# Sigmoid attention with a top-1 mixture of experts on one core: one program order for all engines through attention, and early loads spread over three queues

## The chip, the cores and the metric

The kernel runs on one core of a Trainium2 chip. The metric is the device time of one execution in microseconds (us). The kernel before took 952.7 us, the median of three executions (951.31, 952.70, 954.98). A further execution was taken with the profiler on; all rows of the trace quoted below are from that one.

A core has five engines that run their own instruction streams: TensorE (PE, with its weight loads listed as PEld), VectorE (DVE), ScalarE (ACT), GpSimd (POOL) and SyncE (SP). Each runs its stream in order and waits on semaphores for the others. SP, ACT and POOL can start DMAs; all these DMAs run on the same 16 DMA engines.

## The reference

```
# q, k, v: 8 batches x 12 heads x 448 rows x 64
scores = q @ k.T / sqrt(64) - log(448)
attn   = sigmoid(scores)
x      = (attn @ v), heads side by side: 3584 tokens x 768
# mixture of experts, 8 experts, top 1
logits = x @ w_gate                      # 768 x 8
e      = argmax(logits);  gate = softmax(logits)[e]
out    = gate * (relu(x @ w1[e]) @ w2[e])    # w1: 768 x 1024, w2: 1024 x 768
```

All is float32. Where accuracy matters, a float32 factor is split into a rounded part and its rest ("h" and "l"), and three of the four products are summed.

## The kernel before, in words

**Attention** handles pairs of heads: 8 batches of 6 pairs, 48 pairs. Two pairs make a round of 7 steps (`ST`), so there are 168 steps `s`, and `u, i = divmod(s, 7)`. At an even step, PE runs the products of attention weights and values that are due (`weighted`, L504) and then the scores of two steps (`scores`, L484). Each score tile is turned into attention weights by a sigmoid on ACT (`squash`, L476), four score tiles being in flight. At the end of a round two finished output tiles are copied by ACT and DVE into the pair `xh`, `xl` (L530, L531).

**Loads.** `load_pair` (L429) starts eight DMAs for a pair, four for k and four for q. `load_values` (L445) starts three: the tile `vn` and two pieces of `ve`. `turn` (L457) transposes k or q on DVE. The table `READY` (L541) says at which step of a round each of these is called; loads of k and q are called about twelve steps before use. Rings of tiles (4 for k and for q, 3 for `vn`) bound how far a load can run ahead.

**Gate and tokens.** When a batch's 21 steps (`PB`) are done, its gate is worked out in pieces over the next steps (`gate_a` to `gate_e`), the number of the batch's most frequent expert is read into SP's registers (`load_regs`, L384), and `tokens` (L391) writes the batch's x to the DRAM tensor `x_tok` in two halves of four DMAs, from a staging tile `xt` that has one buffer.

**Experts, first part.** All tokens of a batch are run through that batch's most frequent expert (`moe`, L192). This is 288 matmuls for a batch. From step `START` = 33 on, 14 of them are put among the matmuls of each attention step. The weights come as raw tiles (`wst`, ring of 5, loaded by SP) which ACT rounds (`w1h`, `w2h`) and POOL subtracts (`w1l`, `w2l`); `Weights.ahead(n)` (L171) issues the loads and splits up to part `n`.

**Experts, second part.** The tokens whose own expert is another one are gathered after attention, run through their experts in a loop, and scattered to the output (L628 on).

**What sets the order.** The tile framework normally orders each engine's stream itself, by a model of when things are ready. `tc.manual_schedule(engines=...)` takes engines out of this: their streams keep the order in which the source calls them. Before, PE keeps source order through all of attention, DVE and ACT only up to step 3 (`ORDERED_TO`); after that, DVE, ACT, POOL and SP are ordered by the framework. The work after attention is ordered by the framework up to the last loops.

Of the kernel before, what the change touches and what calls it, by code (L numbers as in the profile page):

```python
# [10 lines left out]
F32 = mybir.dt.float32  # L11
# [4 lines left out]
AF = mybir.ActivationFunctionType  # L16
# [3 lines left out]
P = 128  # L20
NCH = 4
# [4 lines left out]
def tile_sigmoid_attention_top1_moe(  # L26
# [18 lines left out]
    nc = tc.nc  # L45
    B, H, S, D = q.shape
    NT, DM = out.shape
    E = w_gate.shape[1]
    DF = w1.shape[2]
    NP = H // 2  # L50
    KD = DM // P
# [8 lines left out]
    recs = dram.tile([E * NT, 2], U32, name="recs")  # L60

    const = ctx.enter_context(tc.tile_pool(name="const", bufs=1))
# [40 lines left out]

    wgs = const.tile([P, KD, 2 * E], F32R, name="wgs")

    def setup():
        wg = const.tile([P, KD, E], F32, name="wg")
        nc.sync.dma_start(wg, w_gate.rearrange("(t p) e -> p t e", p=P))
        nc.scalar.copy(wgs[:, :, 0:E], wg)
        nc.vector.tensor_sub(wgs[:, :, E : 2 * E], wg, wgs[:, :, 0:E].bitcast(F32))  # L110
        blank = wpool.tile([P, 1024], U32, tag="wst", bufs=RAWS_AHEAD, name="blank")
        blank3 = blank[:, : E * NT // P * 2].rearrange("p (r w) -> p r w", w=2)
        for w, val in enumerate((int(BIG), 0)):
            nc.gpsimd.iota(blank3[:, :, w], pattern=[[0, E * NT // P]], base=val, channel_multiplier=0)
        nc.sync.dma_start(recs.rearrange("(p r) w -> p r w", p=P), blank3)

    def apart(put, puts):
        for other in puts:
# [143 lines left out]
    def gate_b(b):  # L262
        pl = small_ps(b, "pl")
        for c in range(NCH):
            nc.tensor.transpose(
                pl[:, c * 2 * E : (c + 1) * 2 * E], g16[:, c * P : (c + 1) * P], ident[: 2 * E, : 2 * E]
            )
        plv = pl[:, : NCH * 2 * E].rearrange("p (c n e) -> p c n e", n=2, e=E)
        sh = [P, NCH, E]

        def tl(nm, shape=sh, dt=F32):
            return small.tile(shape, dt, tag=nm, name=f"{nm}_{b}")

        def bc(a):
            return a.unsqueeze(2).broadcast_to(sh)

        lg = tl("lg")
        nc.vector.tensor_copy(lg, plv[:, :, 0])
        nc.vector.tensor_add(lg, lg, plv[:, :, 1])
        mx = tl("mx", [P, NCH])  # L280
        nc.vector.tensor_reduce(mx, lg, axis=AX.X, op=ALU.max)
        eq = tl("eq")
        nc.vector.tensor_tensor(eq, lg, bc(mx), op=ALU.is_equal)
        nc.vector.tensor_tensor(eq, eq, rev.unsqueeze(1).broadcast_to(sh), op=ALU.mult)
        mr = tl("mr", [P, NCH])
        nc.vector.tensor_reduce(mr, eq, axis=AX.X, op=ALU.max)
        oh = tl("oh", sh, BF16)
        nc.vector.tensor_tensor(oh, eq, bc(mr), op=ALU.is_equal)
        nc.vector.memset(oh[S - 3 * P :, 3], 0.0)
        z = tl("z")  # L290
        nc.vector.tensor_tensor(z, lg, bc(mx), op=ALU.subtract)
        s1 = tl("s1")
        nc.scalar.activation(s1, z, AF.Sigmoid)
        s2 = tl("s2")
        nc.scalar.activation(s2, z, AF.Sigmoid, scale=-1.0)
        return oh, s1, s2

    def gate_c(b, oh, s1, s2):
        def tl(nm, shape, dt=F32):
            return small.tile(shape, dt, tag=nm, name=f"{nm}_{b}")  # L300

        pc = small_ps(b, "pc")
        nc.tensor.matmul(pc[:, : NCH * E], ones, oh.rearrange("p c e -> p (c e)"), start=True, stop=True)
        cnt = tl("cnt", [P, E])
        nc.vector.tensor_reduce(cnt, pc[:, : NCH * E].rearrange("p (c e) -> p e c", e=E), axis=AX.X, op=ALU.add)
        cm = tl("cm", [P, 1])
        nc.vector.tensor_reduce(cm, cnt, axis=AX.X, op=ALU.max)
        ce = tl("ce", [P, E])
        nc.vector.scalar_tensor_tensor(ce, cnt, cm, rev, op0=ALU.is_equal, op1=ALU.mult)
        cr = tl("cr", [P, 1])  # L310
        nc.vector.tensor_reduce(cr, ce, axis=AX.X, op=ALU.max)
        ri = tl("ri", [P, 1], I32)
        nc.vector.tensor_scalar(ri[:, 0:1], cr, -1.0, float(E), op0=ALU.mult, op1=ALU.add)
        nc.vector.tensor_scalar(ce, ce, cr, None, op0=ALU.is_equal)
        nc.vector.reciprocal(s2, s2)
        nc.vector.tensor_mul(s1, s1, s2)
        sm = tl("sm", [P, NCH])
        nc.vector.tensor_reduce(sm, s1, axis=AX.X, op=ALU.add)
        nc.vector.tensor_scalar(sm, sm, 1e-9, None, op0=ALU.add)
        nc.vector.reciprocal(gates[:, b], sm)  # L320

        nc.vector.tensor_scalar(ce, ce, -1.0, 1.0, op0=ALU.mult, op1=ALU.add)
        lm = tl("lm", [P, NCH, E], BF16)
        nc.vector.tensor_tensor(lm, oh, ce.unsqueeze(1).broadcast_to([P, NCH, E]), op=ALU.mult)
        return ri, lm
# [83 lines left out]
    def small_ps(b, name):  # L409

        return ps_moe.tile([P, 512], F32, tag="moe", name=f"{name}_{b}")
# [17 lines left out]
    def load_pair(g):  # L429
        if g >= NG:  # L430
            return
        b, hp = divmod(g, NP)
        for nm, src in (("k", k), ("q", q)):
            t = apool.tile([P, S // 32, 32], F32, tag=nm + "n", bufs=4, name=f"{nm}n_{g}")
            eng = nc.scalar if (g, nm) == (0, "q") else nc.sync
            for h in range(2):
                for f in range(D // 32):
                    a = 2 * h + f
                    eng.dma_start(  # L439
                        t[32 * a : 32 * (a + 1)],  # L440
                        src[b, 2 * hp + h, :, 32 * f : 32 * (f + 1)].rearrange("(j r) s -> r j s", r=32),
                    )
            ops[g, nm + "n"] = t
# [21 lines left out]
    def warm_up(n):  # L465

        ps = ps_moe.tile([P, 512], F32, tag="moe", name="ps_warm")
        for _ in range(n):
            nc.tensor.matmul(ps[:, :P], ones, ones, start=True, stop=True)
# [61 lines left out]
            nc.vector.tensor_sub(xl, pv[:, :S], xh.bitcast(F32))  # L531
            xch[divmod(g, NP)] = (xh, xl)

    WARM, V_POOL = 76, 3
    START = 33
    PB = NP // 2 * ST
    ET = mybir.EngineType
    ORDERED_TO = 3
    MIX = (7, 7)

    READY = {  # L541
# [7 lines left out]
    def attention():  # L549

        order = ExitStack()
        order.enter_context(tc.manual_schedule(engines={ET.PE}))
        first = order.enter_context(ExitStack())
        first.enter_context(tc.manual_schedule(engines={ET.DVE, ET.Activation}))
        warm_up(WARM)
        load_pair(0)
        load_pair(1)
        turn(0, "k")
        turn(0, "q")
        load_values(0)  # L560
        for g in (2, 3, 4):
            load_pair(g)
        pend_gate = None
        done_av = 0
        for s in range(N_ST + 11 + KD):
            u, i = divmod(s, ST)
            if s == 6:
                setup()
            if s == ORDERED_TO:
                first.close()  # L570
            if s % 2 == 0:


                while done_av < min(s - (s < START), N_ST):
                    weighted(done_av)
                    done_av += 1
                    if done_av % ST == 0:
                        break
                for n in range(s, min(s + 2, N_ST)):
                    scores(n)  # L580
            yield s, MIX[0]
            if i in READY and s < N_ST:
                READY[i](u)
            gb = s - PB
            if gb >= 0:
                b, r = divmod(gb, PB)
                r -= 3 if b == 0 else 2
                at = ("a", "b", None, "c", "l", "d", "e") if b == 0 else ("a", "b", "c", "l", "d", "e")
                what = at[r] if 0 <= r < len(at) else None
                if what == "a":  # L590
                    gate_a(b)
                elif what == "b":
                    pend_gate = gate_b(b)
                elif what == "c":
                    pend_gate = gate_c(b, *pend_gate)
                    gate_out[b] = pend_gate[0]
                elif what == "l":
                    load_regs(b)
                    if b == 0:
                        wts.ahead(2)  # L600
                elif what == "d":
                    gate_d(b, *pend_gate)
                elif what == "e":
                    gate_e(b)
                if 7 <= r < 7 + KD:
                    tokens(b, r - 7)
            yield s, MIX[1]
        order.close()

    wts = Weights([(lambda b=b: regs.get(b)) for b in range(B)])  # L610
# [310 lines left out]
```

## Time and profile before

| what | us |
|---|---|
| median of three executions | 952.7 |
| the profiled execution | 959.16 |
| its span, first to last instruction | 957.4 |
| PE busy in it | 897.4 |
| POOL, ACT, DVE busy | 407.2, 385.7, 350.1 |
| first matmul of the experts (L208) | 96.70 after the start |

The profile has these views: a page with the busy time of each engine and its granted clock over the span; a timeline, in which equal instructions in a row are merged, with the idle time of the engine before them in square brackets and what ended it; groups of instructions with count, busy time and mean; waits by engine, summed, with count and longest; and windows, which give each engine's busy time in chosen stretches, with the granted clock of TensorE as a share of full speed, the mean busy share of the DMA engines and the rate of the data moved. A name such as `at<-sc,bias_s` reads "writes at from sc and bias_s".

### The profile page before, as it was taken

The numbers are of one execution on the slowest core, as the hardware profiler recorded it, in microseconds if no ns is written. First come the engines' busy times: TensorE is split into PE (matmuls) and PEld (weight loads), VectorE is DVE, ScalarE is ACT, GpSimd is POOL, SyncE is SP. The second block draws the span as 40 slices with busy tenths as digits, with TensorE's granted clock in tenths as the row PEclk, the third lists the DMA queues.
The fourth block names the chain that finished last, engine by engine and source line by source line (L and its number), as shares of the span: only waits on it lengthen the run. The fifth ranks groups of instructions, "written<-read, shape, count | busy, mean of one in ns | idle before, by whom it ended". The sixth has DMA issues, their size and how long they took to land.

```text
span 957.4 us, 13357 instructions
## 1 busy us (share of the span) xinstructions
PE 897.4 (94%) x4470; PEld 624.7 (65%) x4470; DVE 350.1 (37%) x730; ACT 385.7 (40%) x690; POOL 407.2 (43%) x362
## 2 busy tenths in 40 slices
PE   9778999999999999997999999999999999997986
PEld 5223667666656767665766766767666678996786
DVE  3335333621352324621334323513352325136354
ACT  4444453325233443343333633435343532313344
POOL 3002431835056523653047613743255508967130
PEclk9778999999999999998999999999999999998898
DMA  9667862755437653955347653946353405529414
GB/s 128 118 121 173 163 155 55 184 122 161 79 90 148 134 137 65 190 100 158 59 112 146 153 116 75 201 106 149 60 150 91 139 1 147 161 56 301 148 43 140
DMA packets 319250, 120.47 MB, mean 126 GB/s; under 512 B 222596, under 2 KB 314212, under 8 KB 319184
## 3 DMA queue, kind: packets, MB, share of 16 engines
q1 hardware_dynamic: 310512, 106.34, 48.2%
q0 software_dynamic: 6816, 13.07, 5.5%
q8 instruction: 35, 0.57, 0.3%
q10 hardware_dynamic: 1856, 0.23, 0.2%
q14 instruction: 31, 0.25, 0.1%
HBM read 97.55 MB, written 24.64 MB: 128 GB/s over the span
## 4 chain that ended last, share of the span: by engine, by line
PE 53%; DMA 7%; DVE 3%; issue 2%; ACT 2%; SPq 1%; POOL 1%; POOLq 0%; DVEq 0%; ACTq 0%
PE ps L229 18%; PE ps L208 12%; PE av L515 6%; PE sc L492 6%; PE ps L797 6%; DMA wst<-in_moe_w_dram 5%; PE psg L256 1%; PE sc L500 1%; PE av L524 1%; DMA x_tok<-xt 1%; DMA w2r<-in_moe_w_dram 1%; DMA w1r<-in_moe_w_dram 1%; SPq L439 1%; POOL w2l L144 0%; ACT w2h L143 0%
## 5 line engine op out<-in xcount | busy, mean ns | idle before, releaser
L478 ACT ACTIVATE at<-sc,bias_s 128x448 f32<-128x448 f32 x336 | 187.6, 636 | 234.9 <-PE sc L492 208.2
L144 POOL TENSOR_TENSOR w2l<-wst,w2h 128x512 fp32r<-128x512 f32 x96 | 123.9, 1307 | 279.1 <-ACT w2h L143 217.6
L144 POOL TENSOR_TENSOR w1l<-wst,w1h 128x768 fp32r<-128x768 f32 x64 | 117.2, 1841 | 158.5 <-ACT w1h L143 157.7
L229 PE MATMUL ps<-hh,w2h 128*128 128x448 f32 x384 | 144.1, 375 | 7.4 <-DVE gt L381 2.7
L208 PE MATMUL ps<-xh,w1h 128*128 128x448 f32 x384 | 142.9, 372 | 8.0 <-DVE hl L214 8.0
L492 PE MATMUL sc<-qt,kt 64*128 64x448 f32 x576 | 141.4, 598 | 5.8 <-ACT at L478 5.3
L515 PE MATMUL av<-at,vn 128*64 128x448 f32 x576 | 134.7, 582 | 12.2 <-DVE xl L531 11.1
L229 PE MATMUL ps<-hl,w2h 128*128 128x448 f32 x384 | 143.4, 373 | 0.0
L229 PE MATMUL ps<-hh,w2l 128*128 128x448 f32 x384 | 142.1, 370 | 0.6 <-POOL w2l L144 0.6
L208 PE MATMUL ps<-xl,w1h 128*128 128x448 f32 x384 | 142.1, 370 | 0.0
L208 PE MATMUL ps<-xh,w1l 128*128 128x448 f32 x384 | 141.8, 369 | 0.0
L492 PEld LDWEIGHTS sc<-qt,kt 64*128 64x128 f32 x576 | 67.7, 254 | 84.1 <-issue 63.1
L214 DVE SCALAR_TENSOR_TENSOR hl<-ps,hh 128x448 fp32r<-128x448 f32 x64 | 39.8, 622 | 196.6 <-ACT hh L213 196.6
L143 ACT CAST w2h<-wst 128x512 fp32r<-128x512 f32 x96 | 57.6, 621 | 99.4 <-PE ps L229 58.7
L229 PEld LDWEIGHTS ps<-hh,w2h 128*128 128x128 f32 x384 | 75.0, 195 | 21.4 <-issue 9.0
L208 PEld LDWEIGHTS ps<-xh,w1h 128*128 128x128 f32 x384 | 72.3, 188 | 23.6 <-DVE hl L214 10.0
L515 PEld LDWEIGHTS av<-at,vn 128*64 128x64 f32 x576 | 37.4, 142 | 76.5 <-issue 52.0
L229 PEld LDWEIGHTS ps<-hh,w2l 128*128 128x128 f32 x384 | 75.0, 195 | 12.0 <-issue 5.5
L229 PEld LDWEIGHTS ps<-hl,w2h 128*128 128x128 f32 x384 | 75.0, 195 | 9.7 <-issue 6.2
L143 ACT CAST w1h<-wst 128x768 fp32r<-128x768 f32 x64 | 53.5, 836 | 68.8 <-DMA wst<-in_moe_w_dram 25.1
L208 PEld LDWEIGHTS ps<-xh,w1l 128*128 128x128 f32 x384 | 72.1, 188 | 13.2 <-issue 7.5
L208 PEld LDWEIGHTS ps<-xl,w1h 128*128 128x128 f32 x384 | 72.4, 189 | 12.6 <-issue 7.1
(148 smaller groups left out, 907.7 us busy)
## 6 DMA issues: line engine op xcount, KB each, us to landing
wst<-in_moe_w_dram SPq DMA_DIRECT2D x64, 384.0 KB
wst<-in_moe_w_dram SPq DMA_DIRECT2D x48, 512.0 KB
kn<-in_k_dram SPq DMA_DIRECT2D x192, 56.0 KB
x_tok<-xt SPq DMA_DIRECT2D x64, 168.0 KB
out_dram<-ob POOLq DMA_DIRECT2D x96, 112.0 KB, 3.2
qn<-in_q_dram SPq DMA_DIRECT2D x188, 56.0 KB
vn<-in_v_dram SPq DMA_DIRECT2D x45, 192.0 KB
w1r<-in_moe_w_dram SPq DMA_DIRECT2D x12, 512.0 KB
```

Of the source, the lines that this page charges most:

```text
L143: nc.scalar.copy(hi, st)
L144: eng.tensor_tensor(lo, st, hi.bitcast(F32), op=ALU.subtract)
L208: nc.tensor.matmul(ps[:, :S], a[:, ws], b_, start=(t == 0 and n == 0), stop=(t == KD - 1 and n == 2))
L214: nc.vector.scalar_tensor_tensor(hl[:, :S], ps[:, :S], 0.0, hh[:, :S].bitcast(F32), op0=ALU.max, op1=ALU.subtract)
L229: nc.tensor.matmul(ps[:, :S], a, b_, start=(j == 0 and n == 0), stop=(j == KF - 1 and n == 2))
L256: nc.tensor.matmul(psg[: 2 * E, :S], wgs[:, t], xch[b, t][n], start=(t == 0 and n == 0), stop=(t == KD - 1 and n == 1),)
L439: eng.dma_start(t[32 * a : 32 * (a + 1)], src[b, 2 * hp + h, :, 32 * f : 32 * (f + 1)].rearrange("(j r) s -> r j s", r=32),)
L478: nc.scalar.activation(at, ps[:, :S], AF.Sigmoid, bias=bias_s, scale=SCALE)
L492: nc.tensor.matmul(pss[h][:, :S], ks, ops[g, "q"][OWN[h]], start=True, stop=True)
L500: nc.tensor.matmul(pss[n][quarter(g, h), :S], ops[g, "k"][OWN[h], KB:], ops[g, "q"][OWN[h]], start=True, stop=True,)
L515: nc.tensor.matmul(psv[g][OWN[h], :S], ops[g, "v"][0][:, h, c, :], ats.pop((g, c, h)), start=(c == 0), stop=False)
L797: nc.tensor.matmul(*a, **kw)
```

## The change

From the start of attention to its end, the streams of all engines keep the order of the source. Around this, some calls change place or engine:

- the gate weights `wg` are loaded by POOL right after the first pair loads are called, and split on POOL (copy and subtract) at step 6; before, SP loaded them at step 6, ACT made the copy and DVE the subtraction;
- the blank records are written by a DMA from POOL in place of SP;
- the two sigmoids of the gate move from `gate_b` to `gate_c`, which is called one or two steps later;
- q of pairs 0 and 1 is loaded from ACT's queue (before: of pair 0);
- values of pairs 0 to 9 are loaded from POOL (before: 0 to 2);
- at step 28 only the first raw weight tiles are loaded (`ahead(0)`), and the first two parts are split at step 32 (`ahead(2)`); before, both stood at step 28.

```diff
+    wg = const.tile([P, KD, E], F32, name="wg")
+
     def setup():
-        wg = const.tile([P, KD, E], F32, name="wg")
-        nc.sync.dma_start(wg, w_gate.rearrange("(t p) e -> p t e", p=P))
-        nc.scalar.copy(wgs[:, :, 0:E], wg)
-        nc.vector.tensor_sub(wgs[:, :, E : 2 * E], wg, wgs[:, :, 0:E].bitcast(F32))
+        nc.gpsimd.tensor_copy(wgs[:, :, 0:E], wg)
+        nc.gpsimd.tensor_sub(wgs[:, :, E : 2 * E], wg, wgs[:, :, 0:E].bitcast(F32))
...
-        nc.sync.dma_start(recs.rearrange("(p r) w -> p r w", p=P), blank3)
+        nc.gpsimd.dma_start(recs.rearrange("(p r) w -> p r w", p=P), blank3)
...
-        s1 = tl("s1")
-        nc.scalar.activation(s1, z, AF.Sigmoid)
-        s2 = tl("s2")
-        nc.scalar.activation(s2, z, AF.Sigmoid, scale=-1.0)
-        return oh, s1, s2
-
-    def gate_c(b, oh, s1, s2):
+        return oh, z
+
+    def gate_c(b, oh, z):
...
+        s1, s2 = tl("s1", [P, NCH, E]), tl("s2", [P, NCH, E])
+        nc.scalar.activation(s1, z, AF.Sigmoid)
+        nc.scalar.activation(s2, z, AF.Sigmoid, scale=-1.0)
...
-            eng = nc.scalar if (g, nm) == (0, "q") else nc.sync
+            eng = nc.scalar if g < Q_ACT and nm == "q" else nc.sync
...
-    WARM, V_POOL = 76, 3
+    WARM, V_POOL, Q_ACT = 76, 10, 2
...
-        order.enter_context(tc.manual_schedule(engines={ET.PE}))
-        first = order.enter_context(ExitStack())
-        first.enter_context(tc.manual_schedule(engines={ET.DVE, ET.Activation}))
+        order.enter_context(tc.manual_schedule())
...
+        nc.gpsimd.dma_start(wg, w_gate.rearrange("(t p) e -> p t e", p=P))
...
-            if s == ORDERED_TO:
-                first.close()
+            if s == START - 1:
+                wts.ahead(2)
...
-                        wts.ahead(2)
+                        wts.ahead(0)
```

More of the change, by code (lines that the diff above doesn't have):

```diff
@@ L532, in weighted @@
             xch[divmod(g, NP)] = (xh, xl)
-    WARM, V_POOL = 76, 3
+    WARM, V_POOL, Q_ACT = 76, 10, 2
     START = 33
     PB = NP // 2 * ST
-    ET = mybir.EngineType
-    ORDERED_TO = 3
     MIX = (7, 7)
```

## The prediction

> **What bounds the kernel now.** I read the page first, for the share of PE.
>
> ```profile
> span 957.4 us, 13357 instructions
> ...
> PE 897.4 (94%) x4470; PEld 624.7 (65%) x4470; DVE 350.1 (37%) x730; ACT 385.7 (40%) x690; POOL 407.2 (43%) x362
> ```
>
> PE sets the time and no other engine is near its limit, so only two things can be won: stretches in which PE has nothing to do, and stretches in which it runs at a lower clock. The windows view, cut at PE's gaps, shows where these lie.
>
> ```profile
> core 0: us, PE busy (x) PEld busy (x) DVE busy (x) ACT busy (x) POOL busy (x), PEclk, DMA share, GB/s
> 0.00:28.40 28.40, 26.36 (x166) 14.41 (x166) 11.30 (x24) 13.08 (x23) 8.11 (x25) 1.00 0.87 126
> 28.40:33.70 5.30, 0.03 (x2) 0.02 (x1) 0.21 (x1) 0.84 (x3) 0.00 (x0) 0.69 0.72 142
> 33.70:59.00 25.30, 25.30 (x114) 9.03 (x114) 7.41 (x13) 15.54 (x30) 0.00 (x0) 0.86 0.59 106
> 59.00:66.00 7.00, 0.07 (x4) 0.04 (x2) 1.22 (x3) 1.57 (x3) 0.00 (x0) 0.65 0.78 158
> 66.00:86.20 20.20, 19.31 (x89) 7.56 (x89) 11.04 (x44) 6.98 (x14) 0.00 (x0) 0.87 0.60 113
> 86.20:96.70 10.50, 6.62 (x21) 2.25 (x21) 3.87 (x7) 5.86 (x11) 6.58 (x6) 0.67 1.11 263
> 96.70:860.00 763.30, 741.37 (x3629) 521.63 (x3628) 267.62 (x571) 302.50 (x544) 358.46 (x305) 0.99 0.52 121
> ```
>
> Ahead of the first expert matmul at 96.7 PE stands still three times, for 4 to 7 us each, and the clock column falls each time. After 96.7 it is idle for only 763.3 - 741.4 = 21.9 us in 763. So the early phase holds the prize. The timeline says who was late in each of the three stops, and what a half clock does.
>
> ```profile
> 8.06 1.84 PE L492 MATMUL sc<-qt,kt 64*128 64x448 f32 x8
> ...
> 30.45 0.48 SPq L108 DMA_DIRECT2D wg<-in_moe_w_gate_dram  x1
> ...
> 32.86 0.23 ACT L109 CAST wgs<-wg 128x48 fp32r<-128x48 f32 x1 [7.22 <-DMA wg<-in_moe_w_gate_dram]
> ...
> 33.68 1.86 PE L492 MATMUL sc<-qt,kt 64*128 64x448 f32 x2 [5.27 <-ACT at L478]
> ...
> 35.47 3.25 PE L515 MATMUL av<-at,vn 128*64 128x448 f32 x8
> ...
> 41.44 1.72 PE L515 MATMUL av<-at,vn 128*64 128x448 f32 x8
> ...
> 64.75 0.65 DVE L400 STREAM_TRANSPOSE xt<-xf 128x448 f32<-128x448 f32 x1 [8.06 <-DMA x_tok<-xt]
> ...
> 65.96 3.26 PE L515 MATMUL av<-at,vn 128*64 128x448 f32 x8 [6.93 <-DVE xl L531]
> ...
> 84.62 3.93 SPq L165 DMA_DIRECT2D wst<-in_moe_w_dram  x5
> ...
> 88.11 0.83 ACT L143 CAST w1h<-wst 128x768 fp32r<-128x768 f32 x1 [3.68 <-DMA wst<-in_moe_w_dram]
> ...
> 90.09 4.75 PE L515 MATMUL av<-at,vn 128*64 128x448 f32 x12 [3.88 <-DVE xl L531]
> ```
>
> All three have one form. An instruction that nobody needs yet was placed ahead of urgent ones and waits for a DMA: on ACT the copy of the gate weights (its load left SP only at 30.45, behind the pair loads), on DVE a token transpose whose staging buffer was still being written out, on ACT the first weight cast. What PE needs (sigmoids, xl) stands behind it. In the first and second stop PE then takes 3.25 and 3.26 us for eight matmuls that take 1.72 us otherwise. The stretches of half clock follow, with two later ones:
>
> ```profile
> 30.42:40.66 10.24, 6.98 (x18) 1.98 (x22) 0.21 (x1) 3.03 (x7) 0.00 (x0) 0.50 0.65 128
> 61.14:71.38 10.24, 5.42 (x14) 1.96 (x16) 4.14 (x7) 0.28 (x1) 0.00 (x0) 0.50 0.73 138
> 88.45:95.28 6.83, 5.19 (x14) 1.75 (x16) 3.87 (x7) 4.94 (x9) 5.16 (x5) 0.50 1.13 255
> 221.57:224.98 3.41, 3.41 (x10) 1.40 (x10) 0.00 (x0) 1.14 (x2) 2.57 (x2) 0.50 1.07 296
> 440.02:446.85 6.83, 5.93 (x16) 2.16 (x18) 1.90 (x3) 1.36 (x3) 3.90 (x3) 0.50 0.83 241
> ```
>
> Half of the PE time in them is loss: 3.5, 2.7 and 2.6 us early, 1.7 and 3.0 later.
>
> **The change, part by part.** *The three early stops.* The wg load is issued at the start, and its two splits stand on POOL, which the windows show idle from 28 to 86 us: ACT and DVE no longer touch them. Token transposes stand at steps 31 to 36 in the source, no longer as early as data allow. The first casts move from step 28 to step 32, while their loads stay at 28. Removed are 5.27 + 3.5, 6.93 + 2.7 and 3.88 + 2.6, together **24.9 us**.
>
> What is late next? Two steps cost PE 1.84 + 1.72 = 3.56 us, so step 32 comes at 8.1 (first scores) + 16 x 3.56 = 65, plus about 4 for the gate's matmuls: 69 us. The five raw tiles are issued about when step 28's register load returns, near 61 to 67; the first landed at most 3.5 us after issue (84.62 to 88.11), so the casts at 69 should find their data. If not, one stop like the third comes back: 6.5 us.
>
> *Queues.* These rows price the loads that move:
>
> ```profile
> 5.46 2.32 SPq L439 DMA_DIRECT2D qn<-in_q_dram  x4
> ...
> 12.94 1.09 PE L492 MATMUL sc<-qt,kt 64*128 64x448 f32 x4 [0.56 <-DVE qt L462]
> ...
> L454 POOL DMA_DIRECT2D ve<-in_v_dram x6 | 3.3, 561 | 0.0
> ...
> L451 POOL DMA_DIRECT2D vn<-in_v_dram x3 | 2.5, 817 | 0.0
> ...
> L144 POOL TENSOR_TENSOR w2l<-wst,w2h 128x512 fp32r<-128x512 f32 x96 | 123.9, 1307 | 279.1 <-ACT w2h L143 217.6 <-PE ps L229 29.2 <-PE pl L265 28.7
> ```
>
> The four DMAs of q for pair 1 leave SP (2.32 us, which every later load of SP gains) for ACT, before the first scores at 8.1 give it a sigmoid to do, so ACT's idleness hides them. PE's one wait for a transposed q, 0.56 us, goes. Seven value loads (pairs 3 to 9) leave SP; on POOL each is 817 + 2 x 561 = 1.94 us, 13.6 us in all, where POOL is idle after its 8.1 us of setup; without that cover they would delay the first weight subtractions. From pair 3 on they queue behind the split of wg, so a late wg holds v of pair 3, which is due near 29 us. The wg and blank-record DMAs join POOL too, about 1 us each by the vn row. The two POOL splits of 128x48 lie between 0 and 1.31 us each (the 128x512 row); I take 0.3, hidden. The sigmoids of the gate (0.2 us each) now come when z is long done.
>
> *After 96.7.* The framework's order costs PE two stops of the same kind; the larger:
>
> ```profile
> 438.42 0.62 ACT L143 CAST w2h<-wst 128x512 fp32r<-128x512 f32 x1 [2.16 <-DMA wst<-in_moe_w_dram]
> ...
> PE ps L208 <- DVE hl L214: 8.0, 5, 4.8
> ...
> ACT w1h L143 <- DMA wst<-in_moe_w_dram: 21.5, 16, 5.8
> ...
> PE ps L229 <- DVE gt L381: 2.7, 2, 1.7
> ...
> PE av L515 <- ACT at L478: 1.1, 2, 0.6
> ```
>
> A cast of a later weight part waits for its load ahead of the relu copy `hh` that PE needs. In source order `hh` of a block stands ahead of the next casts, and w2 casts begin only in the sixth of eight blocks. So the 8.0 us of waits go with half a clock of 1.7 + 3.0: 12.7 us. Against it, source order makes ACT and DVE follow PE closely: at each of the seven expert changes the first cast may wait for a raw tile in front of the sigmoids. The bounds are nothing and a stop like the third (6.5 us) each time. I take the nearer end, about 1 us each by the 1.1 us that PE has waited for sigmoids in all this stretch, though single casts waited up to 5.8: 7 us. And 2 us for DVE, which may stand in line in front of what PE needs once more: about PE's longest wait for a gate piece (1.7). Net **-3.7 us**.
>
> *Sum.* 24.9 + 0.6 + 3.7 = 29.2 us off: the span goes from 957.4 to 928, the profiled execution from 959.16 to 930. The median of the runs lies 6.5 us under the profiled one, which may hold stalls that the others lack; the same 29 off 952.7 gives 923.5. I forecast **924 us**, range of this case 912 to 932.
>
> **The rivals.** *DMA limits the early phase.* Sizes per DMA:
>
> ```profile
> kn<-in_k_dram SPq DMA_DIRECT2D x192, 56.0 KB
> ...
> vn<-in_v_dram SPq DMA_DIRECT2D x45, 192.0 KB
> ...
> ve<-in_v_dram SPq DMA_DIRECT2D x90, 16.0 KB
> ...
> wst<-in_moe_w_dram SPq DMA_DIRECT2D x64, 384.0 KB
> ```
>
> By the new start of the experts (96.7 - 25.5 = 71 us) the queues must have moved 14 pairs of k and q (8 x 56 KB), 11 of v (192 + 32), the blank records and two raw tiles: about 9.9 MB. At the 126 GB/s of the first 28 us that is 79 us, so 8 us of the gain are lost, and the half clock with a stop takes some 3 more: 935. Against it stand 142 to 158 GB/s at a DMA share of 0.72 to 0.78, and 263 with raw tiles. The Trainium skill speaks for this rival: "DMA: Bandwidth & Descriptors", section "Issuing engines are not separate DMA queues", says that DMAs from any engine share the same 16 DMA engines, so spreading issuers saves issue time alone. No row here separates the two; my sum takes only 0.6 us from the spreading.
>
> *Slower: one stop at each expert change.* The chosen expert's number is read late in the step pattern, so its raw tiles start late; with ACT held to source order, the cast sits in front of all sigmoids until they land. If this stops PE as the third early stop did, it costs 6.5 us times 7 changes = 45.5, and the time is 952.7 - 25.5 + 45.5 = 973. It decides from the fourth such stop on (4 x 6.5 = 26). For it: single casts waited 5.8 us. Against it: PE has four score tiles in flight, so a cast must hold ACT for most of two steps (over 9 us with 28 expert matmuls among them) before PE stops.
>
> *All later stops go too.* 21.9 us idle plus 4.7 of half clock vanish with the early 25.5: 900.6. Against it: about half of that idle time is waits for gate pieces and output transposes, which PE's unchanged order sets.
>
> *No gain.* If the expert phase is paced by the loads, an earlier start is paid back by its end: 950 to 957. Against it: DMA share 0.52 over that phase.
>
> **How the numbers follow.** Forecast 0.60; DMA-limited (935, up to 944) 0.17; all later stops gone 0.08; no gain 0.06; slower 0.09. A measurement of this kernel can tell about 0.5% (4.8 us) from no change. Faster by more: 0.60 + 0.17 + 0.08 = 0.85; within: 0.06; slower: 0.09. The range 900 to 946 takes in the first three cases and leaves out the last two, 0.15, and some tails.
>
> **What would show it.** Right: the first L208 matmul near 71 us, no gap over 3 us and full clock before it, no ACT wait for wg, POOL busy with v loads between 10 and 60 us, and no wait of `hl` over 3 us in the middle. Wrong: L208 near 80 with the DMA share near 0.9 (DMA-limited), or ACT's first `w1h` cast of each expert waiting over 5 us with a half clock behind it.

## The result, and the profile after

| | before | after |
|---|---|---|
| median of 4 executions each | 952.63 us | 926.5 us (926.03 to 926.96) |
| ratio | | 0.9723, 95% interval 0.9703 to 0.9743 |
| profiled execution, its span | 959.16, 957.4 us | 926.28, 924.0 us |

In a second measurement of six executions the changed kernel took 926.87 us against 956.1, a ratio of 0.9696 (0.9670 to 0.9722). The prediction was 924 us.

The first lines of the page after the change:

```profile
span 924.0 us, 13302 instructions
PE 881.3 (95%) x4470; PEld 622.4 (67%) x4470; DVE 378.1 (41%) x729; ACT 383.8 (42%) x689; POOL 421.5 (46%) x387
```

PE's busy time fell by 16 us for the same 4470 matmuls: less of it runs at half clock. DVE's rose by 28 us although it lost one instruction; this returns below. The windows view, cut at the first expert matmul and at the first matmul of the second part of the experts (`px`), says where the 33.4 us of span went. First the kernel before, then after. The columns are the stretch, its length, the busy time of PE, PEld, DVE, ACT and POOL with counts, the granted clock, the DMA share and GB/s.

```profile
0.00:96.70 96.70, 77.68 (x389) 33.31 (x390) 35.05 (x91) 43.88 (x82) 14.69 (x31) 0.86 0.75 136
96.70:878.60 781.90, 757.90 (x3702) 536.76 (x3701) 277.31 (x580) 310.50 (x553) 371.75 (x316) 0.99 0.53 124
878.60:957.40 78.80, 61.78 (x383) 54.61 (x381) 37.76 (x60) 31.36 (x57) 20.77 (x16) 0.90 0.37 127
```

```profile
0.00:71.72 71.72, 67.37 (x389) 30.85 (x389) 27.79 (x78) 42.68 (x80) 26.46 (x54) 1.00 0.88 151
71.72:844.00 772.28, 752.54 (x3702) 537.34 (x3701) 312.45 (x593) 310.00 (x554) 374.32 (x318) 0.99 0.54 128
844.00:924.00 80.00, 61.40 (x383) 54.16 (x381) 37.81 (x60) 31.14 (x57) 20.69 (x16) 0.91 0.39 132
```

The early phase lost 25.0 us and runs at full clock throughout, the expert phase lost 9.6, the rest grew by 1.2. The waits view of PE in the expert phase of the changed kernel (who waited for whom: us, times, longest):

```profile
PE ps L208 <- DVE hl L214: 4.4, 2, 4.1
PE ps L208 <- POOL w1l L144: 4.0, 3, 2.1
PE pc L302 <- DVE ob L237: 2.9, 2, 2.7
PE pg L378 <- DVE gm L374: 2.9, 3, 1.6
```

The 8.0 us of waits for `hl` have become 4.4, one stop of 4.1. Waits for `w1l` are new. The longest, 2.1 us, stands right behind the first expert matmul: the first cast now comes late, and POOL's line has the four scatters of the gate ahead of the subtractions.

### The profile page after: what moved, and what is told of

Its sections match the earlier page's. It is cut to its first block, busy times and chain, and to the rows that moved or that the text cites. A ratio compares the mean times of both kernels' runs of the same rounds, so it can differ in the third digit from the quotient of the medians.

```text
span 924.0 us, 13302 instructions
## 1 busy us (share of the span) xinstructions
PE 881.3 (95%) x4470; PEld 622.4 (67%) x4470; DVE 378.1 (41%) x729; ACT 383.8 (42%) x689; POOL 421.5 (46%) x387
## 4 chain that ended last, share of the span: by engine, by line
PE 81%; DMA 3%; DVE 3%; issue 1%; POOL 1%; SPq 1%; ACT 0%; POOLq 0%; DVEq 0%; ACTq 0%
PE ps L208 24%; PE ps L229 24%; PE sc L491 11%; PE av L514 10%; PE ps L793 5%; PE av L523 2%; PE sc L499 2%; PE psg L256 2%; DMA w2r<-in_moe_w_dram 2%; DMA x_tok<-xt 1%; DVE ob L237 1%; POOL w1l L144 1%; DMA w1r<-in_moe_w_dram 0%; DMA kn<-in_k_dram 0%; SPq L403 0%
## 5 line engine op out<-in xcount | busy, mean ns | idle before, releaser
L491 PE MATMUL sc<-qt,kt 64*128 64x448 f32 x576 | 136.8, 586 | 1.2 <-ACT at L477 1.2
L514 PE MATMUL av<-at,vn 128*64 128x448 f32 x576 | 124.8, 552 | 0.0
L398 DVE TENSOR_TENSOR xf<-xh,xl 128x448 f32<-128x448 f32 x48 | 78.3, 1632 | 0.2
L213 ACT ACTIVATE hh<-ps 128x448 fp32r<-128x448 f32 x64 | 35.1, 549 | 95.8 <-PE ps L208 95.8
```

Source lines behind the costliest of these rows:

```text
L213: nc.scalar.activation(hh[:, :S], ps[:, :S], AF.Relu)
L398: nc.vector.tensor_add(xf, xh.bitcast(F32), xl.bitcast(F32))
L491: nc.tensor.matmul(pss[h][:, :S], ks, ops[g, "q"][OWN[h]], start=True, stop=True)
L514: nc.tensor.matmul(psv[g][OWN[h], :S], ops[g, "v"][0][:, h, c, :], ats.pop((g, c, h)), start=(c == 0), stop=False)
```

## The experiments

The runs were taken in three groups, and the kernel before, measured with each, took 956.88, 957.45 and 956.1 us. Since it moves by several us between measurements and the changed kernel hardly does, I compare with the changed kernel (926.5 and 926.87).

**Which phase owes what to the order.** Source order for all engines up to step 33 only:

```diff
+        order.enter_context(tc.manual_schedule(engines={ET.PE}))
+        first.enter_context(tc.manual_schedule(engines={ET.DVE, ET.Activation, ET.Pool, ET.SP}))
...
+            if s == START:
+                first.close()
```

> All edits stay, but the order of the source ends for DVE, ACT, POOL and SP at step 33, where the experts begin; from there the framework orders them as before. My theory (the early gain is order, the middle gain is order too, each in its own phase): first L208 matmul still at 71 to 72 us, the middle loses its 8 us again, so 931 to 935. Rival (order matters only early): 926 to 928.

It took 943.04 us (ratio to before 0.9858, interval 0.9804 to 0.9911). Its windows:

```profile
0.00:71.57 71.57, 67.02 (x390) 30.43 (x390) 28.20 (x80) 43.41 (x81) 26.50 (x54) 1.00 0.90 151
71.57:863.20 791.63, 760.04 (x3701) 537.91 (x3700) 290.36 (x591) 310.75 (x553) 374.42 (x318) 0.99 0.55 126
```

The early gain is all there without the later order. The expert phase takes 791.6 us against 772.3: source order there is worth 19 us once the early phase is short, where I had expected 8 and a time of 931 to 935. In the waits of this kernel PE waits for `hl` again, by more than in the kernel before:

```profile
PE ps L208 <- DVE hl L214: 14.1, 6, 5.0
PE ps L229 <- DVE gt L380: 4.4, 3, 2.4
```

**The edits without the order.** PE in source order, DVE and ACT up to step 3, all moved loads and calls kept:

```diff
-        order.enter_context(tc.manual_schedule())
+        order.enter_context(tc.manual_schedule(engines={ET.PE}))
+        first.enter_context(tc.manual_schedule(engines={ET.DVE, ET.Activation}))
...
+            if s == 3:
+                first.close()
```

> All moved loads, splits and calls stay, but the streams are ordered as before: PE by the source, DVE and ACT by the source up to step 3, the rest by the framework. My theory: only the stop for the gate weights goes (5.3 + 3.5 us) with the 0.6 us of the second q load; the stops at the token transpose and at the first cast return, so about 943, first L208 near 87. Rival (the moved loads alone carry the gain): 926 to 932.

It took 949.94 us in eight executions (946.96 to 952.94), a ratio of 0.9926 (0.9895 to 0.9956), and the first expert matmul came at 90.6: 7 us more and 3.6 us later than I had expected. The stop for the gate weights is gone; those at the token transpose and at the first cast are back. From its timeline:

```profile
50.04 2.68 SPq L403 DMA_DIRECT2D x_tok<-xt  x4
...
56.47 0.65 DVE L399 STREAM_TRANSPOSE xt<-xf 128x448 f32<-128x448 f32 x1 [12.31 <-DMA x_tok<-xt]
...
59.78 3.25 PE L514 MATMUL av<-at,vn 128*64 128x448 f32 x8 [6.56 <-DVE xl L530]
...
81.62 0.83 ACT L143 CAST w1h<-wst 128x768 fp32r<-128x768 f32 x1 [3.11 <-DMA wst<-in_moe_w_dram]
...
83.59 4.75 PE L514 MATMUL av<-at,vn 128*64 128x448 f32 x12 [3.30 <-DVE xl L530]
```

So these two stops are the work of the framework's order alone, and of the 26 to 29 us the edits by themselves give about 7. A stop that I had not expected stands near 25 us: PE waits 2.76 us for `xl`, which the framework placed behind a transpose of q that waited 2.67 us for its load.

**The spread of the loads.** Values of pairs 3 to 9 and q of pair 1 back on SP:

```diff
-    WARM, V_POOL, Q_ACT = 76, 10, 2
+    WARM, V_POOL, Q_ACT = 76, 3, 1
```

> As the changed kernel, but q of pair 1 goes back to SP and values of pairs 3 to 9 go back to SP. My theory: spreading saves issue time alone, 0.6 us: 927, first L208 at 72 to 73. Rival (queue): in source order SP waits for a free vn tile with the k and q loads behind it, so pairs come late and PE stops early on: 932 to 950.

It took 936.43 us (ratio 0.9791, 0.9737 to 0.9844), some 10 us more than the changed kernel; the first expert matmul came at 79.3. The rival's time is right, with one stop, but not its mechanism: SP hardly waited for anything (0.3 us in all between 10 and 33 us), and what came late was the value load itself. In the timeline (SPq is SyncE's line of DMA issues):

```profile
18.60 1.98 SPq L438 DMA_DIRECT2D kn<-in_k_dram  x4
...
29.02 1.99 SPq L438 DMA_DIRECT2D qn<-in_q_dram  x4
31.11 0.41 SPq L450 DMA_DIRECT2D vn<-in_v_dram  x1
...
33.86 1.76 PE L514 MATMUL av<-at,vn 128*64 128x448 f32 x4 [5.52 <-DMA vn<-in_v_dram]
```

The values of pair 3 leave SP at 31.11, behind the pair loads of two microseconds for every four DMAs, and PE needs them at 28.3 (33.86 less the 5.52 of waiting). A stretch of half clock follows. The timeline of the kernel before has the same late load:

```profile
31.63 0.38 SPq L451 DMA_DIRECT2D vn<-in_v_dram  x1
```

There its cost did not show, since PE stood still until 33.68 for the gate weights anyway. Taken together, the two traces say that one stop had two causes at once.

Which of the two moves counts? With q of pair 1 alone back on SP (`Q_ACT` = 1):

> As the changed kernel, but q of pair 1 goes back to SP; the values of pairs 3 to 9 stay on POOL. If the values alone carry what the spread is worth (PE waited 5.5 us for vn without it): within 1 us of the changed kernel. If q counts: 2 to 5 us more.

It took 927.04 us beside 926.87 for the changed kernel: the q load is worth nothing that can be measured.

> The changed kernel itself once more, beside the next three on one chip. 926 to 928.

It took 926.87 us (926.09 to 928.97), as expected.

**The gate weights late again.** Their load by SP at step 6, the splits on ACT and DVE:

```diff
-        nc.gpsimd.tensor_copy(wgs[:, :, 0:E], wg)
-        nc.gpsimd.tensor_sub(wgs[:, :, E : 2 * E], wg, wgs[:, :, 0:E].bitcast(F32))
+        nc.sync.dma_start(wg, w_gate.rearrange("(t p) e -> p t e", p=P))
+        nc.scalar.copy(wgs[:, :, 0:E], wg)
+        nc.vector.tensor_sub(wgs[:, :, E : 2 * E], wg, wgs[:, :, 0:E].bitcast(F32))
...
-        nc.gpsimd.dma_start(wg, w_gate.rearrange("(t p) e -> p t e", p=P))
```

> As the changed kernel, but the gate weights are loaded by SP at step 6 and split by ACT and DVE there, as before. My theory: ACT stands at step 6 (about 17 us) until a load that SP issues behind the pair loads (about 25 us) has landed, a stop like the first one, 5.3 + 3.5 us or more: 935 to 942. Rival (source order alone hides it, ACT gets there late enough): 926 to 928.

It took 942.95 us (ratio 0.9849, 0.9798 to 0.9900), 16 us more than the changed kernel. From its timeline:

```profile
31.28 0.48 SPq L109 DMA_DIRECT2D wg<-in_moe_w_gate_dram  x1
33.56 0.23 ACT L110 CAST wgs<-wg 128x48 fp32r<-128x48 f32 x1 [15.13 <-DMA wg<-in_moe_w_gate_dram]
...
34.38 2.28 PE L524 MATMUL av<-at,ve 64*64 64x448 f32 x8 [12.95 <-ACT at L478]
```

In source order ACT reaches the copy at 18.4 and waits 15 us, twice the wait of the kernel before (7.22). The load left SP at 31.28 here and at 30.45 there, both times behind pair loads: what stands ahead of it in SP's line makes it late. Whether ACT and DVE could keep the splits if the load alone came early was not tried.

**The first casts at step 28.**

```diff
-            if s == START - 1:
-                wts.ahead(2)
...
-                        wts.ahead(0)
+                        wts.ahead(2)
```

> As the changed kernel, but the first two casts stand at step 28 again, right behind the issue of their loads. My theory: ACT waits for the raw tile in front of the sigmoids as before, one stop of 3.9 + 2.6 us: 931 to 934, with a half clock near 65 us. Rival: in source order the four score tiles in flight cover the wait: 926 to 928.

It took 929.07 us (927.53 to 930.75), about 2 more than the changed kernel, with a range that overlaps that of its second measurement (926.09 to 928.97): between the two theories. The trace shows the stop:

```profile
64.89 0.83 ACT L143 CAST w1h<-wst 128x768 fp32r<-128x768 f32 x1 [0.49 <-DMA wst<-in_moe_w_dram]
...
66.54 0.83 ACT L143 CAST w1h<-wst 128x768 fp32r<-128x768 f32 x1 [0.82 <-DMA wst<-in_moe_w_dram]
...
69.55 0.58 PE L378 MATMUL pg<-gm,same 128*128 128x16 f32 x2 [3.87 <-DVE gm L374]
```

The raw tiles had nearly landed (0.49 and 0.82 us of waiting, 3.68 in the kernel before), but the casts still pushed `xh`, `xl` and DVE's `gm` back. PE waits 3.87 us for `gm` in place of 1.17, a half clock follows, and the first expert matmul comes 4.8 us later (76.5). Part returns: the wait for `w1l` behind it, 2.1 us in the changed kernel, is gone.

**DVE's longer instruction.** One line of DVE grew by 39 us, the sum `xf` of two tiles in SBUF for the tokens; all others together fell by 11. Groups of before and after (count, then busy us and mean ns):

```profile
L399 DVE TENSOR_TENSOR xf<-xh,xl 128x448 f32<-128x448 f32 x48 | 39.3, 819 | 1.6
```

```profile
L398 DVE TENSOR_TENSOR xf<-xh,xl 128x448 f32<-128x448 f32 x48 | 78.3, 1632 | 0.2
...
L530 DVE TENSOR_TENSOR xl<-av,xh 128x448 fp32r<-128x448 f32 x48 | 27.6, 617 | 44.8 <-ACT xh L529 44.7
```

Sorted by the trace, 30 of the 48 after the change lie for over 0.1 us beside one of POOL's TENSOR_TENSOR instructions and take 2.25 us in the mean; the 18 others take 0.59. `xl`, of the same size but with one operand in PSUM, takes 0.62 either way, and so do the transposes of k and q. The longest stop left stands near such an `xf`:

```profile
784.56 5.43 POOL L144 TENSOR_TENSOR w1l<-wst,w1h 128x768 fp32r<-128x768 f32 x3
784.59 5.90 DVE L398 TENSOR_TENSOR xf<-xh,xl 128x448 f32<-128x448 f32 x1
...
786.44 0.37 SPq L136 DMA_DIRECT2D wst<-in_moe_w_dram  x1
...
786.86 2.83 SPq L403 DMA_DIRECT2D x_tok<-xt  x4
...
792.97 0.65 DVE L399 STREAM_TRANSPOSE xt<-xf 128x448 f32<-128x448 f32 x1 [2.49 <-DMA x_tok<-xt]
...
794.18 0.74 PE L208 MATMUL ps<-xh,w1h 128*128 128x448 f32 x1 [4.14 <-DVE hl L214]
```

One `xf` lasts as long as three subtractions of POOL in a row. The expectations below take it for the cause of the stop, but the rows say otherwise. `hl` stands in DVE's line behind the transpose at 792.97, and that waited another 2.49 us after `xf` had ended, until the staging tile was written out. Those writes left SP only from 786.86 on, behind a weight load that had waited 5.8 us for a raw tile, until the first of the three subtractions ended. A short `xf` would have left DVE waiting for the same writes: the stop is of the same kind as the second early one.

The stretch itself is a second matter. The Trainium skill, "GPSIMD Engine Reference", section "1. Specifications", says that GpSimd's SBUF interfaces are shared with VectorE and names as contention DVE instructions in a two-port mode or with two SBUF inputs. The trace agrees as far as `xf`, with two inputs in SBUF, goes. I tried one operand, in a kernel that leaves the rest `xl` out of the tokens:

```diff
-        nc.vector.tensor_add(xf, xh.bitcast(F32), xl.bitcast(F32))
+        nc.vector.tensor_scalar(xf, xh.bitcast(F32), 0.0, None, op0=ALU.add)
```

> As the changed kernel, but DVE makes the token tile xf from the rounded part xh alone, an instruction with one operand in SBUF in place of two; the rest xl is left out of the tokens written for the second part of the experts. Theory A (GpSimd's subtractions, which read two operands in SBUF, stretch a DVE instruction that does the same): xf takes 0.6 us each in place of a mean of 1.63, DVE busy 378 falls to about 330, the stop of 4.1 us with half clock near 790 goes: 917 to 922. Theory B (the stretch has another cause, such as the DMAs beside it): xf stays at 1.6, 926.

It took 926.86 us: no change. Its `xf`, by duration in ns (least, median, most), and the same line of the changed kernel:

```profile
L398 DVE TENSOR_SCALAR xf<-xh x48: 349/776/6633, 67.6 to 793.7; 128x448 f32<-128x448 f32 x48
```

```profile
L398 DVE TENSOR_TENSOR xf<-xh,xl x48: 581/766/6598, 67.7 to 795.8; 128x448 f32<-128x448 f32 x48
```

Two operands are not needed: the one-operand form is faster alone (0.35 us) and is held up as long (6.6). The time is Theory B's, but not its cause: 31 of 48 lie beside POOL again, at 2.03 us against 0.37, and all of those over 0.7 us are among them. What both forms share is that they read and write SBUF alone; but so do the transposes, which are never held up. Of the two conditions that the page names, the sum meets the second; that the one-operand form meets the first, a two-port mode, would fit its 0.35 us, but no run isolates it. Nor can this run price the stretch, since it didn't remove it. The stop near 790 is there as before, 4.31 us, with DVE waiting 2.83 us for the writes of the staging tile.

The sum on POOL in place of DVE:

```diff
-        nc.vector.tensor_add(xf, xh.bitcast(F32), xl.bitcast(F32))
+        nc.gpsimd.tensor_add(xf, xh.bitcast(F32), xl.bitcast(F32))
```

> As the changed kernel, but POOL makes xf in place of DVE. Theory A: no DVE instruction is stretched any more; POOL takes about 1.1 us each (1.3 us for 512 columns), 54 us more, and has room at 46% busy: 917 to 924. Theory B: POOL's line gets longer right where each expert's first weights are split, PE waits for w1l: 928 to 940.

It took 933.67 us (931.83 to 934.57), 7 more. DVE's work fell to 301.6 us, yet PE waited more, in the expert phase for `hl` 6.8 us and for `qt` 1.8: DVE now waits in line for POOL (125.9 us before `xt`, up to 11.9 at a time), and what PE needs stands behind that. The longest of these waits, 11.9 us, ends in a stop of 5.2 us at `hl`, near the same place as before.

**Without xf.** The tokens are transposed from the output tile in PSUM as soon as a pair is done, two pairs to a staging tile, two tiles in place of one:

```diff
+            nc.vector.transpose(xt[:, :, n, :], pv[:, :S].rearrange("p (j s) -> p j s", s=32))
+        b, hp = divmod(2 * u, NP)
+        rows = x_tok[b * S : (b + 1) * S].rearrange("(j r) (i f) -> i r j f", r=32, i=4)
+        for i in range(4):
+            nc.sync.dma_start(rows[i][:, :, hp * 32 : (hp + 2) * 32], xt[32 * i : 32 * (i + 1)].rearrange("r j t s -> r j (t s)"))
...
-                if 7 <= r < 7 + KD:
-                    tokens(b, r - 7)
```

> As the changed kernel, but the tokens are transposed straight from the attention output in PSUM when a pair is done, two pairs to a staging tile with two buffers, and xf goes altogether. Theory A: DVE loses 78 us of work and its two-operand instructions, the stop near 790 goes, x_tok is written earlier: 915 to 921. Theory B: the writes of the first batch now fall into the first 70 us, where the DMA engines are 0.88 busy, and the longer stay in PSUM holds the next output tile: first L208 at 75 us or later, 926 to 935.

It took 921.99 us (918.95 to 923.63), and once more, beside the changed kernel:

> The kernel with the tokens transposed straight from PSUM, once more beside the changed kernel. If dropping xf is a gain: 4 to 7 us under the changed kernel. Else the same.

920.49 us (918.36 to 923.79), ratio to before 0.9630 (0.9600 to 0.9659), 6.4 us under the changed kernel with no overlap of the two ranges. This is the best version found. Its windows:

```profile
0.00:75.16 75.16, 69.15 (x390) 31.24 (x390) 29.29 (x81) 42.84 (x80) 29.18 (x56) 0.98 0.91 160
75.16:839.90 764.74, 749.94 (x3701) 535.47 (x3700) 233.26 (x541) 309.84 (x554) 367.73 (x316) 1.00 0.55 129
```

Both theories hold in part: the early phase pays 3.4 us (75.2 against 71.7), the expert phase gains 7.5, and PE waits for `hl` no more in it. The edit drops `xf`, adds a second staging tile and writes the tokens earlier, all at once. The stop that went had ended with a wait for the staging tile; what dropping `xf` alone is worth is not shown. The early loss shows in PE's list as one wait for `gm` of 2.24 us, 1.17 in the changed kernel, and 3.41 us of half clock behind it.

**A gate piece later.** With that version, `gate_e` one step later for every batch:

```diff
-("a", "b", None, "c", "l", "d", "e") if b == 0 else ("a", "b", "c", "l", "d", "e")
+("a", "b", None, "c", "l", "d", None, "e") if b == 0 else ("a", "b", "c", "l", "d", None, "e")
```

> The same, and the last piece of the gate (gate_e) one step later for every batch, so that its matmul no longer waits for DVE's gm (2.2, 1.6, 1.0 us in three places). Theory: 3 to 4 us less than without that. Rival: the expert matmul behind it waits for the same tile ring instead, no change.

It took 933.98 us, 13.5 more: a clear miss. PE's waits for `gm` in the expert phase, 3.5 us with a longest of 1.6 in the version without this edit, became:

```profile
PE pg L378 <- DVE gm L374: 11.5, 4, 4.5
```

The longest of them in the timeline:

```profile
161.43 3.75 POOL L144 TENSOR_TENSOR w2l<-wst,w2h 128x512 fp32r<-128x512 f32 x3
...
162.98 3.88 DVE L374 TENSOR_TENSOR gm<-gates,block 128x16 f32<-128x16 f32 x1
...
165.13 1.69 POOL L239 TENSOR_TENSOR ob<-ob,gt 128x896 f32<-128x896 f32 x1
...
167.00 0.58 PE L378 MATMUL pg<-gm,same 128*128 128x16 f32 x2 [4.47 <-DVE gm L374]
```

`gm` is a product of two small tiles in SBUF that takes 0.13 us alone. One step later it falls among POOL's subtractions and is held up as `xf` was: 3.88, 3.83 and 3.37 us in three of eight cases, each beside POOL's two-operand instructions. Here PE waits for the very instruction that is held up. Each of the three stops (4.47, 2.88 and 3.43 us) drew a half clock after it.

## Why the prediction was right or wrong

- *Time.* 924 forecast, 926.5 measured, inside the case's range of 912 to 932. The terms, taken against the profiled execution, gave a span of 928; it was 924.0. The median lies above its forecast and the span below, because the profiled execution of the kernel before lay 6.5 us above its median, while that of the changed kernel lies at its median; which waits the other executions of the kernel before lack, the runs don't show. Against the 29.2 us of the forecast, 26.1 came off in the first measurement, 29.2 in the second and 33.4 between the profiled spans, so the near hit says less than the terms do.
- *The early stops, 24.9 us.* Right as a sum: the first expert matmul came at 71.72 (forecast 71), the phase 25.0 us shorter, with no stop over 3 us and full clock. Each mechanism was shown by putting it back: the token transpose returns with the framework's order (6.56 us of waiting), the gate weights with a late load (12.95), the first cast with its old place (3.87).
- *The queues, 0.6 us.* The step that failed. "My sum takes only 0.6 us from the spreading" left out what became late next once the first stop was gone: the value load of pair 3, in the same place of SP's line. I asked that question of the third stop only. The spread of the values carries about 8 us of the early gain; q, to which the 0.6 belonged, carries none. That the early sum came out right is luck in this part: I credited the first stop to the gate weights alone, and the change happened to move the value load too. The Trainium skill, "DMA: Bandwidth & Descriptors", section "Issuing engines are not separate DMA queues", says that spreading the issuers saves issue time only. The trace agrees: with 2 us of issue for every four DMAs ahead of this load in SP's line, PE waited 5.5 us for it.
- *The third stop, 6.5 us.* Right in kind, too large for the changed order: put back, it costs about 2 us, since the raw tiles land sooner after their issue than before and the wait for `w1l` goes in exchange. Under the framework's order it is back at 3.30 us of waiting with a half clock.
- *After 96.7, net 3.7 us.* Mis-sized: the expert phase lost 9.6 and the rest grew by 1.2, net 8.4. Of the 9 us that I gave back, the 7 for casts in front of the sigmoids did not come: in all of it ACT waited 6.4 us for `wst`, 58.3 before (21.5 + 36.8), and no wait of PE for a sigmoid stands in PE's list. The 2 us for DVE were too few: the stop of 4.14 us for `hl`, behind a transpose that waits for the staging tile, came with 6.83 us of half clock, in which PE was busy for 5.87, so about 7 us in all. My sign "no wait of `hl` over 3 us" failed there. In this phase PE's idle time fell by 4.3 us and its busy time by 5.4; I haven't traced every part of that. The stretch of `xf` I had not seen in the rows of before, though its mean of 819 ns stood there beside 618 for `xl`.
- *The rivals.* DMA did not limit the early phase: it moved 151 GB/s at a share of 0.88 where I had feared 126. The stop at every expert change did not come. Not all later stops went.

## What to carry to other kernels

When a stall goes, look up what else was late at that moment: a wait hides every other wait that ends before it, and each is uncovered in turn. In an in-order stream a call's cost is what stands behind it, so loads and preparations belong where the engine's line is free of urgent work, and moving one call by a step can cost more than what it avoids. An engine at 40% busy can still set the end, when its line stands in front of what the busiest engine needs. And where a long instruction and a wait stand one behind the other in such a line, the wait that ends last is the cause, not the instruction that looks odd.

## What the runs showed of the hardware that I had not expected

Some DVE instructions on SBUF alone are held up by GpSimd's two-operand instructions, by the whole length of several in a row: `xf` takes 0.59 us alone, 2.25 in the mean beside them, 6.6 at most, and the small `gm` 0.13 alone and up to 3.88, while DVE's transposes and its full-width instructions with an operand in PSUM keep their 0.6 to 0.65. It cost PE time where PE's operand was the held-up result (`gm`) or stood behind it. And short stops are enough to draw a half clock: after one of 2.75 us in the changed kernel, from 244.55 on, the windows view shows 3.41 us of it, while the one of 2.13 us that ended at 74.53 drew none. The stop of 2.75 us, too, stands behind held-up instructions in DVE's line: four small ones of the gate, beside POOL's subtractions, that take 0.78, 1.22, 0.97 and 1.08 us in place of 0.19 each.

```profile
247.09:250.50 3.41, 3.20 (x10) 2.44 (x11) 3.17 (x12) 0.00 (x0) 2.88 (x3) 0.50 0.33 53
```
